# A product of h moved to GpSimd and four casts of v moved to ScalarE in a fused retention and bilinear feed-forward kernel

## The chip, the core and the metric

The kernel runs on one core of a Trainium2 chip. The metric is device time in microseconds (us) of one execution. The five engines run their own instruction streams and meet through semaphores: TensorE (PE in the rows, with its weight loads as PEld), VectorE (DVE), ScalarE (ACT), GpSimd (POOL) and the queue of SyncE (SP), which issues DMA transfers here.

## The reference

```python
gamma = 1.0 - 2.0 ** (-5.0 - np.arange(H))         # q, k, v: 4 x 8 heads x 768 x 64
for t in range(S):
    state = gamma * state + outer(k[t], v[t])
    y[t] = q[t] @ state / sqrt(D)
x = y.transpose(0, 2, 1, 3).reshape(3072, 512)
out = ((x @ w_a) * (x @ w_b)) @ w_out              # w_a, w_b: 512 x 1536, w_out: 1536 x 512
```

Inputs and output are float32. The kernel multiplies in bf16 and accumulates in float32.

## The kernel before, in words

**Slots.** The 3072 rows of x are 24 slots of 128 tokens, six per batch. For a slot, GpSimd scales k and q by a decay table (`kqb`, line 292) and SP transposes the result by DMA (`kqT`, line 333). The cast of v to bf16 is `vb`; GpSimd does it for most slots (line 251), ScalarE for slots 12 to 19 (`v_cast`, line 249). `turn(new, old)` takes slots in pairs: the state update (`st`, line 394, reads `kqb` and `vb`), the scores (`at`, line 376, masked by VectorE into `aT`, line 382), and, for the older pair, the two products that give y (lines 414 and 424), which ScalarE copies to `xt` (line 435).

**Tiles.** The feed-forward part takes the slots in seven tiles, J = 0 to 6, of 4, 2, 2, 2, 2, 4 and 8 slots. For a tile, `xt` meets twelve blocks `ft` of 128 columns of w_a and of w_b. A plain block (`ffn_a`, `ffn_g`) takes four matmuls into a PSUM bank `a`, which ScalarE copies to `asb` (line 575), and four into a bank `g`; VectorE then multiplies `g` by `asb` into `ht` (line 586), which is h. The banks come from a ring of three in strict rotation, which the scores of one slot of a pair also use, so the first product of the block behind a turn takes the bank of the `g` ahead of it. The product of h with w_out, and some of the first products, are done in a Strassen-like form with seven half products p1 to p7 instead of eight: class `Group` for w_out (banks mA, mB, mC, sums of h in `hs`), `Unit` for the last tile, and `Quad` for the sixth.

**The sixth tile** is J = 5, slots 14 to 17. Its blocks 0, 6 and 1, 7 are two "halved pairs". Pair p = 0 is `a` (w_a) and `b` (w_b), pair p = 1 is `c` and `d`. A half product leaves its bank through `Quad.leave`. For w_a, VectorE adds the bank to a saved copy (`snapf`, line 965) and writes `asb`. For w_b, it adds likewise into `ht` and then multiplies `ht` by `asb` in place. That last multiplication goes to VectorE for i = 0 (once per pair, in p2) and to GpSimd for i = 1 (twice per pair, in p5 and p4). Blocks 2 and 3 are plain ones (F2, G2, F3, G3).

**Order.** Everything is issued in the order of the code, each engine in its own order. The sixth tile's pairs stand in a string, `LACED`, between the halved w_out product of tile 4 (the `m` steps). Around the place of the change it reads

```python
... V18 L20 m3 c1 d1 F3 H3 c2 d2 c6 d6 c7 d7 c5 d5 m4 c3 d3 V19 c4 d4 G3
```

`V18` is `v_cast(18)`, and `L20` is `late_v(20)`, GpSimd's casts of v of slots 20 and 21. `H3` is a sum of h. Behind the string come `late_kq(22)` (the scaled k and q of slots 22 and 23), `turn(18, 16)`, blocks 4, 5 and 8, `turn(20, 18)`, blocks 9, 10 and 11, `turn(22, 20)`, and `big()`, the last tile. The sums of h for the sixth tile's w_out product are named by three digits, s, a and b: `hsum(5, s, a, b)`. `sums(5, ft)` issues those that belong behind block ft (`WHEN`): "324" behind block 4, "102", "402" and "346" behind block 5, "224d" and "124" behind 9, "424" behind 10, and "246", "146", "446" behind 11. `blocks(J, a, b)` calls it for all blocks but its last one; "324" goes to VectorE, the others to GpSimd (a "d" means VectorE). `weight_pieces` are sums of weight blocks for the last tile (`wsa`, `wsb`) on GpSimd.

Of the kernel before, what the change touches and what calls it, by code (L numbers as in the profile page):

```python
# [12 lines left out]
ALU = mybir.AluOpType  # L13
# [9 lines left out]
       "S02 S01 b7 a2 b2 S04 a6 b6 S13 a5 b5 S12 a3 b3 a4 b4 S11 c7 d7 c6 d6 S14 c5 d5 "  # L23
       "c3 c4 d4 d3")
V_LATE = range(12, 20)
LACED = ("X3 X2 m1 m7 m2 a1 b1 a2 b2 m6 X1 a6 b6 a7 b7 F2 X4 m5 a5 b5 K20 G2 a3 b3 a4 b4 V18 L20 "
         "m3 c1 d1 F3 H3 c2 d2 c6 d6 c7 d7 c5 d5 m4 c3 d3 V19 c4 d4 G3")
LOADS = "p0 p1 w0 w1 a1 b1 a2 k2 q2 b2 v2 o0 o1 o2 o3 o4 o5 s6 t8".split()

# [2 lines left out]
def kernel(  # L32
# [10 lines left out]
    nc = tc.nc  # L43
# [7 lines left out]
    NFT = DFF // P  # L51
# [51 lines left out]
    def seq(bi):  # L103
        ins = bi.ins
        prev = last.get(ins.engine)
        if prev is not None:
            tc.add_manual_dep(ins, prev.name, nosync, reason="program order")
        last[ins.engine] = ins
        return bi
# [5 lines left out]
    raws, wst, whole = {}, {}, {}  # L115

    def load_slot(t, names="kqv"):
        b, ci = divmod(t, NCH)
        for nm in names:
            src = {"k": k, "q": q, "v": v}[nm]  # L120
            if nm == "q":
                if t % 2 == 0:
                    load_two(nm, src, b, ci // 2, t)
                continue
            if t % 2 == 0:
                whole[nm] = raw_tile([P, 2, H, D], F32, nm + "f", nm + "f")
            raws[nm, t] = whole[nm][:, t % 2]
            s = src[b, :, ci * P : (ci + 1) * P, :].rearrange("h p d -> p h d")
            seq(nc.sync.dma_start(out=raws[nm, t], in_=s))
# [117 lines left out]
    def cast(engine, dst, src):  # L247
        if engine is nc.scalar:
            seq(nc.scalar.copy(dst, src))
        else:  # L250
            seq(engine.tensor_copy(dst, src))  # L251
# [19 lines left out]
    kb, qb, vb, kqT, aT = {}, {}, {}, {}, {}  # L271
# [27 lines left out]
    def casts(t, between=lambda: None):  # L299
        new_nat(t)  # L300
        scaled(nc.gpsimd, t, 0)
        between()
        scaled(nc.gpsimd, t, 1)
        if t not in range(12, 20):
            cast(nc.gpsimd, vb[t], raws["v", t])
        u = t + 2
        if u == 20:
            load_slot(u, "kq")
        flip(t)
        if u == 20:  # L310
            load_slot(u + 1, "k")
            return
        if u == 21:
            load_slot(u - 1, "v")
            load_slot(u, "v")
            load_slot(22, "kq")
            return
        if u in V_LATE:
            if u == 13:
                load_slot(12, "q")  # L320
            elif u == 19:
                load_slot(18, "kq")
            load_slot(u, {12: "k", 18: ""}.get(u, "kq"))
            if u % 2:
                load_slot(u - 1, "v")
                load_slot(u, "v")
        elif u < NSLOT:
            load_slot(u)
# [8 lines left out]
    def late_kq(t):  # L337
# [5 lines left out]
        if t == 20:  # L343
            load_slot(23, "k")
            load_slot(22, "v")
            load_slot(23, "v")

    def late_v(t):
        for u in (t, t + 1):
            cast(nc.gpsimd, vb[u], raws["v", u])  # L350

    def casts_two(t):
        for u in (t, t + 1):
# [74 lines left out]
    def leave(t):  # L428
        J, i = where[t]
        key, i = (J, i) if J < BIG else ((J, i // 4), i % 4)  # L430
        if i == 0:
            pool, tag = (wstage, "w") if key == (BIG, 1) else (xtp, "xt")
            xt[key] = pool.tile([P, KT, 4 * P], BF16, tag=tag, name="xt")
        for r in range(2):
            seq(nc.scalar.copy(xt[key][:, 2 * r : 2 * r + 2, i * P : (i + 2) * P],
                               ys[t // 2][r].rearrange("p j a s n -> p j (a s n)")))
# [127 lines left out]
    def ffn_a(J, ft, c0=0, c1=None):  # L564
        c1 = TILES[J] * P if c1 is None else c1
        if J not in ht:
            ht[J] = htp.tile([P, NFT, 4 * P], BF16, tag="ht", name="ht")
        fs = slice(ft * P, (ft + 1) * P)
        bank = psff.tile([P, 4 * P], F32, tag="ff", name="a")
        a = bank[:, : c1 - c0]  # L570
        for kt in range(KT):
            seq(nc.tensor.matmul(a, wa_bf[:, kt, fs], xcols(J, kt, c0, c1),  # L572
                                 start=(kt == 0), stop=(kt == KT - 1)))
        asb = asbs[J, ft, c0] = asbp.tile([P, 4 * P], BF16, tag="asb", name="asb")[:, : c1 - c0]
        seq(nc.scalar.copy(asb, a))  # L575
        psff.back(bank)

    def ffn_g(J, ft, c0=0, c1=None):
        c1 = TILES[J] * P if c1 is None else c1
        fs = slice(ft * P, (ft + 1) * P)  # L580
        bank = psff.tile([P, 4 * P], F32, tag="ff", name="g")
        g = bank[:, : c1 - c0]
        for kt in range(KT):
            seq(nc.tensor.matmul(g, wb_bf[:, kt, fs], xcols(J, kt, c0, c1),  # L584
                                 start=(kt == 0), stop=(kt == KT - 1)))
        seq(nc.vector.tensor_tensor(ht[J][:, ft, c0:c1], g, asbs.pop((J, ft, c0)), op=ALU.mult))  # L586
        psff.back(bank)

    def ffn_ab(J, ft):
        store()  # L590
        ffn_a(J, ft)
        ffn_g(J, ft)
# [3 lines left out]
    def store():  # L596
        for dst, src in held:
            seq(nc.sync.dma_start(out=dst, in_=src))
        held.clear()
# [21 lines left out]
    def tt(dst, x, y, op, eng=nc.vector):  # L621
        seq(eng.tensor_tensor(dst, x, y, op=op))  # L622
# [23 lines left out]
    def hsum(J, s, a, b, eng=nc.vector):  # L646
        U = slice(int(J == 0), 2 if isinstance(J, tuple) else TILES[J] // 2)
        hs_tile(J, s)
        v = ht[J].rearrange("p (k j) (u r n) -> p r k j u n", k=2, r=2, n=P)
        A11, A12, A21, A22 = (v[:, r, k2, a:b, U] for r in range(2) for k2 in range(2))  # L650
        S = {x: hs[J, x][:, a:b, U] for x in (1, 2, 3, 4) if (J, x) in hs}
        x, y, op = {3: (A11, A21, ALU.subtract), 2: (A22, S[3], ALU.subtract), 1: (A21, A22, ALU.add),
                    4: (A12, S.get(2), ALU.subtract)}[s]
        tt(S[s], x, y, op, eng)
# [8 lines left out]
    def sums(J, ft, eng=nc.vector):  # L663
        for what in WHEN.get(ft, []):
            hsum(J, *map(int, what[:3]), nc.vector if what[3:] else eng)
# [105 lines left out]
    def laced(order):  # L771
        made = {"m": Group(4, 0, Y0, AT0, Y1)}
        for p in range(2):
            made.update({"ac"[p]: Quad(p, "a", AT1, "kqT2"), "bd"[p]: Quad(p, "b", Y1, "aT")})
        ht[5] = htp.tile([P, NFT, 4 * P], BF16, tag="ht", name="ht")
        for x in order.split():
            if x[0] == "H":
                hsum(5, int(x[1]), 0, 1)
            elif x[0] in "XFGVKL":
                {"X": xf_sum, "F": lambda f: (store(), ffn_a(5, f)), "G": lambda f: ffn_g(5, f), "V": v_cast,  # L780
                 "K": late_kq, "L": late_v}[x[0]](int(x[1:]))
            else:
                getattr(made[x[0]], "p" + x[1])()

# [147 lines left out]
    class Quad:  # L932
# [40 lines left out]
        def leave(self, i, c, bank, n):  # L973
            cols = slice(c * DH, (c + 1) * DH)
            if self.w == "a":
                tt(self.half(i)[:, cols], self.bank[bank], self.snaps[n], ALU.add)
                return
            h = ht[5][:, NP * i + self.p, cols]
            tt(h, self.bank[bank], self.snaps[n], ALU.add)
            tt(h, h, self.half(i)[:, cols], ALU.mult, nc.vector if i == 0 else nc.gpsimd)  # L980

        def p1(self):
            self.A = self.whole(FF)
# [64 lines left out]
    D_, G_, A_ = nc.vector, nc.gpsimd, nc.scalar  # L1048
    K, Q = 0, 1
# [75 lines left out]
    def blocks(J, a, b):  # L1125
        for ft in range(a, b):
            ffn_ab(J, ft)
            if J == 5 and ft + 1 < b:
                sums(J, ft, G_ if ft > 8 else nc.vector)
        if J == 5 and b == 6:  # L1130
            sums(J, 5, G_)

# [7 lines left out]
    def v_cast(t):  # L1140
        cast(nc.scalar, vb[t], raws["v", t])
# [26 lines left out]
    weight_pieces(4)  # L1168
    casts(11)
    blocks(2, 3, 6)  # L1170
    hsum(2, 3, 0, 6, G_)
    blocks(2, 6, 7)
    turn(8, None)
    casts(12, lambda: three(2, 7))
    hsums(2, 0, 3, G_)
    blocks(2, 10, 11)
    turn(10, 8)
    blocks(2, 11, NFT)
# [38 lines left out]
    hsums(4, 3, 6, G_)  # L1217
    casts(19)
    laced(LACED)
    hsum(5, 3, 1, 2, G_)  # L1220
    hsum(5, 2, 0, 2, G_)
    late_kq(22)
    turn(18, 16)
    late_v(22)
    blocks(5, 4, 6)
    blocks(5, 8, 9)
    weight_pieces(2)
    turn(20, 18)
    sums(5, 8, G_)
    blocks(5, 9, NFT)  # L1230
    turn(22, 20)
    sums(5, NFT - 1, G_)
    weight_pieces(8)
# [31 lines left out]
```

## Time and profile before

| | |
|---|---|
| time, median of 3 runs | 219.09 us (218.52 to 219.52) |
| time of the profiled execution | 218.49 us |
| its span, first to last instruction | 216.8 us |
| granted TensorE clock | 1.00 throughout |
| busy: PE, DVE, ACT, POOL | 97%, 69%, 47%, 72% of the span |
| chain that ended last | 89% PE |

The profiled execution's time is 1.69 us more than its span, and 0.60 us below the median. In the timeline rows the columns are the start in us, the busy time from the first start to the last end of the instructions that the row merges, the engine, the line, the operation, what is written and read, the shape, and the count. Matmuls overlap, since a new one starts while the one ahead is still draining. Two of 256 columns are shown with 0.38 us, though the next pair starts 0.22 us after them. So a wait of TensorE is read from the distance of starts, not from the busy time.

### The profile page before, as it was taken

To read this page: it belongs to the slowest core of one execution; us is meant where nothing else is said; L and a number is where in the kernel's file an instruction comes from. 1 tells how busy PE (TensorE), PEld (TensorE's weight loads), DVE (VectorE), ACT (ScalarE), POOL (GpSimd) and SP (SyncE) were. 2 spreads that over 40 slices of the span, in tenths; PEclk is the share of its full clock that TensorE was granted. 3 is DMA by queue.
4 is the path that set the end of the run, shared out by engine and by line. 5 is a ranking of instruction groups with operands and counts; after the bars stand their busy time and mean duration, and the time that the engine had idled before them with its cause. 6 is when DMAs were issued, how large, how long until landed. Compare 5 with 4: busy or idle time off the path is not lost.

```text
span 216.8 us, 5705 instructions
## 1 busy us (share of the span) xinstructions
PE 210.4 (97%) x2240; PEld 146.4 (68%) x2252; DVE 149.2 (69%) x273; ACT 102.8 (47%) x231; POOL 155.4 (72%) x187
## 2 busy tenths in 40 slices
PE   7989999999999999999999999999999999999994
PEld 3558445587458888888888877456864444458883
DVE  3776346845984486356377979686577987688962
ACT  3256325343224444465576475446546656652331
POOL 5265876879776849989879979999997999530000
DMA  5999999999999999999979999960013000000055
GB/s 162 290 321 364 384 317 358 384 266 232 186 237 246 197 238 223 197 206 275 200 148 261 243 207 210 243 131 3 3 52 143 0 0 3 2 0 0 27 194 169
DMA packets 85162, 39.68 MB, mean 183 GB/s; under 512 B 57488, under 2 KB 78864, under 8 KB 85136
## 3 DMA queue, kind: packets, MB, share of 16 engines
q1 hardware_dynamic: 84992, 39.26, 78.1%
q8 instruction: 17, 0.28, 0.5%
q10 hardware_dynamic: 144, 0.07, 0.1%
q14 instruction: 9, 0.07, 0.1%
HBM read 28.31 MB, written 6.29 MB: 160 GB/s over the span
## 4 chain that ended last, share of the span: by engine, by line
PE 89%; SPq 3%; DMA 3%; DVE 1%; issue 1%; ACT 1%; POOL 0%; ACTq 0%
PE a L572 18%; PE g L584 18%; PE mA L689 12%; PE uA L863 9%; PE mB L689 6%; PE o L609 5%; PE uB L863 4%; SPq L138 3%; DMA wsta<-in_moe_w_a_dram 3%; PE mC L689 3%; PE at L376 2%; PE uC L863 2%; PE y L424 2%; PE st L394 2%; PE fa L953 2%; PE fb L953 1%
## 5 line engine op out<-in xcount | busy, mean ns | idle before, releaser
L586 DVE TENSOR_TENSOR ht<-g,asb 128x256 bf16<-128x256 f32 (+1 forms) x70 | 34.4, 493 | 31.1 <-PE g L584 28.0
L572 PE MATMUL a<-xt,wa_bf 128*128 128x256 bf16 (+1 forms) x277 | 48.4, 299 | 0.2
L584 PE MATMUL g<-xt,wb_bf 128*128 128x256 bf16 (+1 forms) x279 | 48.2, 300 | 0.1
L575 ACT CAST asb<-a 128x256 bf16<-128x256 f32 (+1 forms) x70 | 30.0, 429 | 34.8 <-PE a L572 33.2
L584 PEld LDWEIGHTS <-wb_bf 128*128 128x128 bf16 x280 | 27.0, 98 | 10.2
L572 PEld LDWEIGHTS <-wa_bf 128*128 128x128 bf16 x280 | 26.5, 98 | 10.7 <-POOL wa_bf L251 0.4
L292 POOL TENSOR_TENSOR kqb<-kf,ktab 128x512 bf16<-128x512 f32 x22 | 23.3, 1062 | 7.2 <-DMA kf<-in_k_dram 4.3
L870 ACT COPY snap<-uA 128x512 f32<-128x512 f32 x36 | 20.0, 588 | 15.4 <-PE uA L863 13.0
L689 PEld LDWEIGHTS <-hs 128*128 128x128 bf16 x234 | 22.8, 98 | 3.6
L292 POOL TENSOR_TENSOR kqb<-qf,qtab 128x512 bf16<-128x512 f32 x18 | 19.2, 1065 | 4.8 <-DMA qf<-in_q_dram 4.8
L382 DVE TENSOR_TENSOR aT<-at,mask 128x512 bf16<-128x512 f32 x36 | 22.3, 682 | 0.3
L622 POOL TENSOR_TENSOR ht<-gsb,asb 128x512 bf16<-128x512 bf16 x13 | 15.2, 1173 | 7.0 <-DVE gsb L622 6.9
L696 ACT COPY snaps<-mA 128x256 f32<-128x256 f32 x30 | 11.0, 374 | 18.9 <-PE mA L689 18.9
L689 PEld LDWEIGHTS <-ht 128*128 128x128 bf16 x180 | 17.5, 98 | 3.2
L622 POOL TENSOR_TENSOR hs<-ht 128x384 bf16<-128x384 bf16 (+3 forms) x14 | 15.8, 1132 | 2.1 <-DVE ht L586 2.1
L622 POOL TENSOR_TENSOR hs<-ht,hs 128x384 bf16<-128x384 bf16 (+1 forms) x17 | 16.8, 994 | 0.6 <-DVE ht L586 0.5
L689 PE MATMUL mA<-wsum,hs 128*128 128x256 bf16 x120 | 15.2, 273 | 0.0
L251 POOL CAST vb<-vf 128x512 bf16<-128x512 f32 x16 | 9.8, 633 | 6.7 <-DMA vf<-in_v_dram 6.7
L622 DVE TENSOR_TENSOR osb<-mB,snaps 128x256 f32<-128x256 f32 x20 | 8.4, 421 | 8.2 <-ACT snaps L696 4.4
L609 PE MATMUL o<-wo_bf,ht 128*128 128x512 bf16 x46 | 10.6, 379 | 0.1
L622 DVE TENSOR_TENSOR gsb<-uB,snap 128x512 bf16<-128x512 f32 x12 | 8.2, 686 | 2.9 <-ACT snap L870 2.1
L622 DVE TENSOR_TENSOR asb<-uB,snap 128x512 bf16<-128x512 f32 x12 | 8.2, 685 | 2.9 <-ACT snap L870 2.0
(138 smaller groups left out, 373.4 us busy)
## 6 DMA issues: line engine op xcount, KB each, us to landing
qf<-in_q_dram SPq DMA_DIRECT2D x12, 512.0 KB, 6.1
out_dram<-osb SPq DMA_DIRECT2D x21, 256.0 KB, 4.2
kf<-in_k_dram SPq DMA_DIRECT2D x18, 256.0 KB, 5.0
vf<-in_v_dram SPq DMA_DIRECT2D x18, 256.0 KB, 5.1
wsta<-in_moe_w_a_dram SPq DMA_DIRECT2D x6, 512.0 KB, 7.7
wsto<-in_moe_w_out_dram SPq DMA_DIRECT2D x6, 512.0 KB, 8.7
wstb<-in_moe_w_b_dram SPq DMA_DIRECT2D x5, 512.0 KB, 8.3
kf<-in_k_dram SPq DMA_DIRECT2D x3, 512.0 KB, 7.1
```

Source lines behind the costliest of these rows:

```text
L292: seq(eng.tensor_tensor(dst, src, tab, op=ALU.mult))
L382: seq(nc.vector.tensor_tensor(aT[t][:, r], at[r], mask.to_broadcast([P, HP, P]), op=ALU.mult))
L572: seq(nc.tensor.matmul(a, wa_bf[:, kt, fs], xcols(J, kt, c0, c1), start=(kt == 0), stop=(kt == KT - 1)))
L575: seq(nc.scalar.copy(asb, a))
L584: seq(nc.tensor.matmul(g, wb_bf[:, kt, fs], xcols(J, kt, c0, c1), start=(kt == 0), stop=(kt == KT - 1)))
L586: seq(nc.vector.tensor_tensor(ht[J][:, ft, c0:c1], g, asbs.pop((J, ft, c0)), op=ALU.mult))
L609: seq(nc.tensor.matmul(o, ht[J][:, ft, i * P : (i + 1) * P], wo_bf[:, ft], start=(ft == 0), stop=(ft == NFT - 1), skip_group_check=True))
L622: seq(eng.tensor_tensor(dst, x, y, op=op))
L689: seq(nc.tensor.matmul(m, w, right[:, j], start=(first and j == 0), stop=(j == NP - 1), skip_group_check=True))
L696: seq(nc.scalar.copy(self.snaps[:, n], self.bank["A"]))
L863: seq(nc.tensor.matmul(m, w, right[:, k], start=(first and k == 0), stop=(k == 1), skip_group_check=True))
L870: seq(nc.scalar.copy(self.snaps[n], self.bank["A"]))
```

## The change

One multiplication moves from VectorE to GpSimd: that of `d2`, the step p2 of pair p = 1 for w_b. Four casts of v, slots 20 to 23, move from GpSimd to ScalarE, each behind the copy of one plain block (4, 5, 9 and 11). To make room for the calls, `blocks(5, 4, 6)` and `blocks(5, 9, NFT)` are cut in two, which moves the sum "324" from behind block 4 to behind block 5, behind the calls of the three sums of block 5.

```diff
-LACED = ("... K20 G2 a3 b3 a4 b4 V18 L20 "
+LACED = ("... K20 G2 a3 b3 a4 b4 V18 "
          "m3 c1 d1 F3 H3 c2 d2 c6 d6 c7 d7 c5 d5 m4 c3 d3 V19 c4 d4 G3")
...
-    def late_v(t):
-        for u in (t, t + 1):
-            cast(nc.gpsimd, vb[u], raws["v", u])
...
             h = ht[5][:, NP * i + self.p, cols]
             tt(h, self.bank[bank], self.snaps[n], ALU.add)
-            tt(h, h, self.half(i)[:, cols], ALU.mult, nc.vector if i == 0 else nc.gpsimd)
+            tt(h, h, self.half(i)[:, cols], ALU.mult, nc.vector if (i, self.p) == (0, 0) else nc.gpsimd)
...
+        if (J, b) == (5, 10):
+            sums(J, 9, G_)
         if J == 5 and b == 6:
             sums(J, 5, G_)
...
     late_kq(22)
     turn(18, 16)
-    late_v(22)
-    blocks(5, 4, 6)
+    blocks(5, 4, 5)
+    v_cast(20)
+    blocks(5, 5, 6)
+    sums(5, 4)
+    v_cast(21)
     blocks(5, 8, 9)
     weight_pieces(2)
     turn(20, 18)
     sums(5, 8, G_)
-    blocks(5, 9, NFT)
+    blocks(5, 9, 10)
+    v_cast(22)
+    blocks(5, 10, NFT)
+    v_cast(23)
     turn(22, 20)
```

VectorE's order from the step c2 to the step d4. Before, `ht<-ht,asb` is the product of d2, and the two rows ahead of it are the additions of c2 and d2:

```order
L622 TENSOR_TENSOR asb<-fa,snapf 128x256
L622 TENSOR_TENSOR ht<-fa,snapf 128x256
L622 TENSOR_TENSOR ht<-ht,asb 128x256
L622 TENSOR_TENSOR asb<-fa,snapf 128x256
L622 TENSOR_TENSOR ht<-fb,snapf 128x256
L622 TENSOR_TENSOR osb<-mB,snaps 128x256
L622 TENSOR_TENSOR ht<-fb,asb 128x256
```

With the change (its lines stand four lower in number here):

```order
L618 TENSOR_TENSOR asb<-fa,snapf 128x256
L618 TENSOR_TENSOR ht<-fa,snapf 128x256
L618 TENSOR_TENSOR asb<-fa,snapf 128x256
L618 TENSOR_TENSOR ht<-fb,snapf 128x256
L618 TENSOR_TENSOR osb<-mB,snaps 128x256
L618 TENSOR_TENSOR ht<-fb,asb 128x256
```

The product is gone, so the additions of c5 and d5 follow those of c2 and d2 at once.

GpSimd's order over the same steps and up to the sums of block 5, before (the first row is the last of the scalings of slots 20 and 21):

```order
L292 TENSOR_TENSOR kqb<-qf,qtab 128x2x4x64
L622 TENSOR_TENSOR ht<-ht,asb 128x256
L251 CAST vb<-vf 128x512 x2
L622 TENSOR_TENSOR ht<-ht,asb 128x256 x2
L622 TENSOR_TENSOR hs_2601<-ht 128x256
L622 TENSOR_TENSOR hs_2662<-ht,hs_2601 128x512
L292 TENSOR_TENSOR kqb<-kf,ktab_175 128x2x4x64
L292 TENSOR_TENSOR kqb<-qf,qtab 128x2x4x64
L292 TENSOR_TENSOR kqb<-kf,ktab_175 128x2x4x64
L292 TENSOR_TENSOR kqb<-qf,qtab 128x2x4x64
L251 CAST vb<-vf 128x512 x2
L622 TENSOR_TENSOR hs_2803<-ht 128x512
```

and with the change:

```order
L292 TENSOR_TENSOR kqb<-qf,qtab 128x2x4x64
L618 TENSOR_TENSOR ht<-ht,asb 128x256 x4
L618 TENSOR_TENSOR hs_2599<-ht 128x256
L618 TENSOR_TENSOR hs_2660<-ht,hs_2599 128x512
L292 TENSOR_TENSOR kqb<-kf,ktab_175 128x2x4x64
L292 TENSOR_TENSOR kqb<-qf,qtab 128x2x4x64
L292 TENSOR_TENSOR kqb<-kf,ktab_175 128x2x4x64
L292 TENSOR_TENSOR kqb<-qf,qtab 128x2x4x64
L618 TENSOR_TENSOR hs_2799<-ht 128x512
```

The four casts are gone, and one product more stands behind that of b4.

VectorE's order from block 4 to the turn behind block 8, before (`hs_2601<-ht` is the sum "324"):

```order
L586 TENSOR_TENSOR ht<-g,asb 128x512
L622 TENSOR_TENSOR hs_2601<-ht 128x512
L586 TENSOR_TENSOR ht<-g,asb 128x512 x2
L382 TENSOR_TENSOR aT<-at_2835,mask 128x512
L382 TENSOR_TENSOR aT<-at_2836,mask 128x512
```

and with the change:

```order
L582 TENSOR_TENSOR ht<-g,asb 128x512 x2
L618 TENSOR_TENSOR hs_2599<-ht 128x512
L582 TENSOR_TENSOR ht<-g,asb 128x512
L378 TENSOR_TENSOR aT<-at_2833,mask 128x512
L378 TENSOR_TENSOR aT<-at_2834,mask 128x512
```

The sum now stands between the products of blocks 5 and 8.

More of the change, by code (lines that the diff above doesn't have):

```diff
@@ L25 @@
 V_LATE = range(12, 20)
-LACED = ("X3 X2 m1 m7 m2 a1 b1 a2 b2 m6 X1 a6 b6 a7 b7 F2 X4 m5 a5 b5 K20 G2 a3 b3 a4 b4 V18 L20 "
+LACED = ("X3 X2 m1 m7 m2 a1 b1 a2 b2 m6 X1 a6 b6 a7 b7 F2 X4 m5 a5 b5 K20 G2 a3 b3 a4 b4 V18 "
          "m3 c1 d1 F3 H3 c2 d2 c6 d6 c7 d7 c5 d5 m4 c3 d3 V19 c4 d4 G3")
@@ L778, in laced @@
                 hsum(5, int(x[1]), 0, 1)
-            elif x[0] in "XFGVKL":
+            elif x[0] in "XFGVK":
                 {"X": xf_sum, "F": lambda f: (store(), ffn_a(5, f)), "G": lambda f: ffn_g(5, f), "V": v_cast,
-                 "K": late_kq, "L": late_v}[x[0]](int(x[1:]))
+                 "K": late_kq}[x[0]](int(x[1:]))
             else:
```

## Prediction

> **What bounds the kernel now.** I read the page first, then the busy time by stage, then the timelines of the engines around the change.
>
> ```profile
> span 216.8 us, 5705 instructions
> PE 89%; SPq 3%; DMA 3%; DVE 1%; issue 1%; ACT 1%; POOL 0%; ACTq 0%
> 10.00:120.00 110.00, 109.33 (x1359) 81.41 (x1359) 70.34 (x130) 51.11 (x120) 86.25 (x102) 1.00 1.15 263
> 120.00:150.00 30.00, 29.77 (x384) 19.84 (x387) 24.71 (x46) 16.44 (x39) 28.12 (x32) 1.00 0.90 179
> 150.00:213.60 63.60, 63.28 (x442) 40.63 (x446) 48.57 (x78) 32.17 (x67) 36.94 (x37) 1.00 0.12 42
> ```
>
> The second line is the chain that ended last: 89% of the span is TensorE's own work, and GpSimd holds 0% of it. The stage rows (length, then PE, PEld, DVE, ACT, POOL busy) say the same by place. The change acts between 120 and 150 us. There TensorE is busy for 29.77 of 30.00 us, while GpSimd is at 28.12 and VectorE at 24.71. From 150 us to the last product TensorE is at 63.28 of 63.60. So relief for GpSimd or VectorE is worth only what TensorE waits for them. GpSimd looks full, but that alone costs nothing.
>
> Busy time can hide short waits, so I looked for them in the distances of TensorE's starts.
>
> ```profile
> 131.15 0.38 PE L953 MATMUL fa<-xt,wea 128*128 128x256 bf16 x2
> 131.37 0.38 PE L953 MATMUL fb<-xt,web 128*128 128x256 bf16 x2
> 131.72 0.38 PE L953 MATMUL fa<-xf,wa_bf 128*128 128x256 bf16 x2
> 132.04 0.38 PE L953 MATMUL fb<-xf,wb_bf 128*128 128x256 bf16 x2
> ...
> 130.22 1.10 DVE L622 TENSOR_TENSOR ht<-ht,asb 128x256 bf16<-128x256 bf16 x1
> 131.25 0.41 DVE L622 TENSOR_TENSOR asb<-fa,snapf 128x256 bf16<-128x256 f32 x1
> 131.59 0.41 DVE L622 TENSOR_TENSOR ht<-fb,snapf 128x256 bf16<-128x256 f32 x1
> ```
>
> A pair of half products takes 0.22 us: 131.15 to 131.37. But c4 starts 0.35 us after d3 (131.37 to 131.72) and d4 another 0.32 us later: waits of 0.13 and 0.10, together 0.23 us. Both reuse a bank that VectorE still has to read. The read for c4 ends at 131.25 + 0.41 = 131.66, that for d4 at 131.59 + 0.41 = 132.00, each some 0.05 us ahead of the product. VectorE is late there because of the product of d2 in the row at 130.22, the one that the change takes away. I found no other wait of TensorE of this kind up to the end; what is left are steps of about 0.1 us where the shape of the products changes.
>
> **The change, part by part.**
>
> *The product of d2.* VectorE loses the row at 130.22 with its 1.10 us.
>
> ```profile
> 130.45 0.37 ACT L965 COPY snapf<-fa 128x256 f32<-128x256 f32 x1 [0.23 <-PE fa L953]
> 130.72 0.38 ACT L965 COPY snapf<-fb 128x256 f32<-128x256 f32 x1
> ```
>
> The addition of c5 then waits for ScalarE's copy instead, which ends at 130.82; that of d5 for 131.10. So the reads end near 130.87 + 0.41 = 131.28 and 131.21 + 0.41 = 131.62. Without waits c4 would start at 131.59 and d4 at 131.81. Both reads are done by then, with 0.31 and 0.19 us to spare, so the whole 0.23 us goes. What is late next is ScalarE's copy, which follows TensorE at a fixed distance and doesn't hold it.
>
> *The product on GpSimd.*
>
> ```profile
> 130.14 1.04 POOL L292 TENSOR_TENSOR kqb<-qf,qtab 128x512 bf16<-128x512 f32 x1
> 131.14 0.71 POOL L622 TENSOR_TENSOR ht<-ht,asb 128x256 bf16<-128x256 bf16 x1
> 131.80 1.17 POOL L251 CAST vb<-vf 128x512 bf16<-128x512 f32 x2
> 132.93 1.30 POOL L622 TENSOR_TENSOR ht<-ht,asb 128x256 bf16<-128x256 bf16 x2
> 138.46 1.04 POOL L292 TENSOR_TENSOR kqb<-kf,ktab 128x512 bf16<-128x512 f32 x1 [0.37 <-DMA kf<-in_k_dram]
> 139.47 1.04 POOL L292 TENSOR_TENSOR kqb<-qf,qtab 128x512 bf16<-128x512 f32 x1
> 140.45 1.17 POOL L251 CAST vb<-vf 128x512 bf16<-128x512 f32 x2
> 141.58 1.16 POOL L622 TENSOR_TENSOR hs<-ht 128x512 bf16<-128x512 bf16 x1
> ```
>
> The product takes about 0.65 us here (1.30 for two) and stands at 131.80 in place of two casts, which held 1.13 us up to the next start. So what follows comes some 0.5 us earlier, until the scaling at 138.46, which waits for a load of k and does not move. At 140.45 the other two casts go, and the sums start there instead of 141.58, 1.13 us earlier. Queued behind the product are those of d5 and d4, two sums and the scalings of slots 22 and 23, none of them later than before. GpSimd's lead is worth nothing by the stage rows: TensorE waits for it nowhere. I count 0.
>
> *The casts on ScalarE.* Here is the engine they move to, with the copies that they stand behind or ahead of.
>
> ```profile
> 131.83 0.62 ACT L249 CAST vb<-vf 128x512 bf16<-128x512 f32 x1
> 136.08 0.59 ACT L575 CAST asb<-a 128x512 bf16<-128x512 f32 x1
> 137.81 0.59 ACT L575 CAST asb<-a 128x512 bf16<-128x512 f32 x1 [1.14 <-PE a L572]
> 139.48 0.59 ACT L575 CAST asb<-a 128x512 bf16<-128x512 f32 x1 [1.08 <-PE a L572]
> 142.99 0.59 ACT L575 CAST asb<-a 128x512 bf16<-128x512 f32 x1
> 144.66 0.59 ACT L575 CAST asb<-a 128x512 bf16<-128x512 f32 x1 [1.09 <-PE a L572]
> 146.39 0.59 ACT L575 CAST asb<-a 128x512 bf16<-128x512 f32 x1 [1.14 <-PE a L572]
> 148.29 0.37 ACT L249 CAST gst<-st 128x256 bf16<-128x256 f32 x1 [1.32 <-PE st L394]
> ...
> 140.24 0.32 PE L394 MATMUL st<-vb,kqb 128*64 128x64 bf16 x8
> 147.94 0.32 PE L394 MATMUL st<-vb,kqb 128*64 128x64 bf16 x8
> ```
>
> A cast takes 0.62 us and falls into idle time of 1.14, 1.08, 1.09 and 1.32 us ahead of the next instruction, so it ends about 0.5 us before that one is due. If that cover were gone, the rest of the cast would push the copy, and with it the product of the block. Their data is there: GpSimd read v of slots 20 and 21 from 131.80 on, of 22 and 23 from 140.45 on, and ScalarE comes to them after about 136.7, 138.4, 143.6 and 147.0. Their readers are the state updates at 140.24 and 147.94, after casts that end near 137.3 and 139.0 for the one, near 144.2 for the other; slot 23 is read later still. Cost 0.
>
> The Trainium skill (SBUF — State Buffer, section "Who interferes with whom") says that ScalarE waits for no other engine at its SBUF ports; the 0.62 us above, taken while GpSimd casts from 131.80, agrees.
>
> *The sum "324".* It moves behind the product of block 5 on VectorE.
>
> ```profile
> 137.57 0.80 DVE L622 TENSOR_TENSOR hs<-ht 128x512 bf16<-128x512 bf16 x1
> 138.69 0.69 DVE L586 TENSOR_TENSOR ht<-g,asb 128x512 bf16<-128x512 f32 x1 [0.32 <-PE g L584]
> 140.41 0.69 DVE L586 TENSOR_TENSOR ht<-g,asb 128x512 bf16<-128x512 f32 x1 [1.03 <-PE g L584]
> 141.86 1.04 PE L572 MATMUL a<-xt,wa_bf 128*128 128x512 bf16 x3
> 144.66 0.58 DVE L622 TENSOR_TENSOR hs<-ht,hs 128x512 bf16<-128x512 bf16 x1
> ```
>
> It took 0.80 us, and the room between the two products is 140.41 − 138.69 − 0.69 = 1.03. Its reader is the sum at 144.66, 5 us later. GpSimd's scaling from 138.46 to 139.50 stands beside it. The pair at 130 shows what that does: VectorE's product began at 130.22 under GpSimd's row from 130.14 to 131.18 and ended at 131.32, 0.14 us after it. So "324" may end as late as about 139.5 + 0.3 = 139.8, still ahead of the product of block 8, due at 140.41 − 0.23 = 140.18. Cost 0, with the far end below as a rival. No DMA and no queue of SP changes its order.
>
> **Sum.** −0.23 + 0 + 0 + 0 = −0.23 us. Against the profiled execution: 218.49 − 0.23 = 218.26. That execution lies 0.60 below the median of 219.09, so as a median 218.86. Bounds of the terms: the gain lies between 0 (below) and 0.3, if the steps of 0.1 us near it shrink too.
>
> **Rivals.**
>
> *A. Nothing arrives.* The 0.23 us is met again by the next wait, for a bank, a mask or the load of k at 138.46. A turn, with its masks and banks, follows right behind d4 and G3. Against it: no TensorE distance up to the end is longer than its shape asks for, so nothing stands ready to take it. Time 218.49, as a median 219.09.
>
> *B. GpSimd's lead counts.* If TensorE waited for sums of h that GpSimd brings 1.13 us earlier, the gain would be 0.23 + 1.13 = 1.36 us: 217.13, as a median 217.73. For it: GpSimd is busy for 28.12 of 30 us. Against: 0% of the chain, and 63.28 of 63.60 behind it.
>
> *C. "324" is locked out (slower).* From 138.46 on GpSimd runs without a pause: scalings to 139.50 and 140.51, then, with the change, sums to about 141.6 and 142.7. If VectorE lost against each new one, "324" would end near 139.8, 140.8, 141.9 or 143.0, and the product of block 8 about 0.65 later. TensorE's row at 141.86, due at 141.63, takes that product's bank. One or two losses cost nothing, and three decide: 142.53 − 141.63 = +0.9, net +0.67 (as a median 219.76). Four cost +2.0, net +1.8 (220.9). Against it: the product at 130.22 got in after one GpSimd instruction.
>
> The Trainium skill (the same page and section) states the lock as a rule: a VectorE instruction with two SBUF inputs and a GpSimd one that reads SBUF shut each other out, and the second waits for the whole of the first. The row at 130.22 agrees; by that rule as it stands, one loss is the likely case and C costs nothing.
>
> *D. A cause that the rows don't show*, such as a stall in fetching instructions on engines whose streams change length: +1.2 or more, 220.3 or above.
>
> **How the numbers follow.** Chances: the forecast 0.69, A 0.12, B 0.07, C 0.08 (0.03 at three losses, 0.05 at four or more), D 0.04. About 0.5% (1.1 us) is what a measurement of this kernel can tell from no change. Within it lie the forecast, A and C at three: 0.84. Faster by more: B, 0.07. Slower by more: C at four and D, 0.09. The three runs shown reach from 0.57 below their median to 0.43 above it. The forecast with that spread is 218.3 to 219.3, A 218.5 to 219.5, C at three 219.8. The range 218.0 to 219.7 holds the first two whole, with some tenths for another chip, and leaves out B, D and most of C, fewer than 2 in 10.
>
> **What would show it.** Right: c4 and d4 start 0.22 us after the product ahead; the last product ends 0.2 us earlier; "324" ends before 140.2; ScalarE's copies of blocks 5, 8, 10 and 11 keep their distance to TensorE. Wrong: a TensorE row behind a turn that starts late with VectorE's product just ahead of it (C), a hole in GpSimd's or ScalarE's stream that no semaphore explains (D), or TensorE rows from 150 on that close up by more than 0.3 us (B).

## The result, and the profile after

The changed kernel takes 218.27 us (median of 20 runs, 218.16 to 218.52), against 218.81 us for the kernel before in as many runs (218.34 to 219.52). The ratio is 0.9974, with a 95% interval of 0.9966 to 0.9982. It is faster by a quarter of a per cent, which lies within the 0.5%. The profiled execution took 218.28 us with a span of 216.6.

So two numbers have to be explained. The median fell by 0.54 us. The shortest run fell by 0.18 and the profiled span by 0.2, about the 0.23 us of the prediction. The rest of the median goes with the spread: 9 of the 20 runs before were above 218.9 us, none of the changed kernel's. Such longer executions are what the experiments are about.

The stages of the changed kernel, in the columns of the prediction's first rows (length, then PE, PEld, DVE, ACT, POOL busy):

```profile
120.00:150.00 30.00, 29.98 (x389) 20.02 (x388) 23.74 (x45) 18.51 (x43) 27.49 (x29) 1.00 0.91 179
150.00:213.60 63.60, 63.49 (x446) 40.52 (x444) 48.35 (x79) 32.28 (x67) 36.16 (x37) 1.00 0.12 43
```

VectorE has 1.0 us less, GpSimd 0.6 less and ScalarE 2.1 more between 120 and 150 us. (The trace of before lacks some records of TensorE, 384 products against 389, so its busy time isn't compared.)

The timeline of TensorE and VectorE at the place of d2's product, after:

```profile
131.39 0.38 PE L949 MATMUL fb<-xt,web 128*128 128x256 bf16 x2
131.61 0.38 PE L949 MATMUL fa<-xf,wa_bf 128*128 128x256 bf16 x2
131.83 0.38 PE L949 MATMUL fb<-xf,wb_bf 128*128 128x256 bf16 x2
...
129.79 0.41 DVE L618 TENSOR_TENSOR ht<-fa,snapf 128x256 bf16<-128x256 f32 x1
130.88 0.42 DVE L618 TENSOR_TENSOR asb<-fa,snapf 128x256 bf16<-128x256 f32 x1 [0.67 <-ACT snapf L961]
131.22 0.41 DVE L618 TENSOR_TENSOR ht<-fb,snapf 128x256 bf16<-128x256 f32 x1
```

c4 and d4 (second and third row) each start 0.22 us behind the product ahead, and VectorE now waits for ScalarE's copy, as forecast. Set row against row, TensorE is 0.02 us later than before up to d3, 0.11 earlier at c4, 0.22 earlier at d4, and 0.22 earlier at every row from there to the end.

GpSimd, ScalarE and the moved sum, after:

```profile
131.18 2.65 POOL L618 TENSOR_TENSOR ht<-ht,asb 128x256 bf16<-128x256 bf16 x4
138.40 1.04 POOL L292 TENSOR_TENSOR kqb<-kf,ktab 128x512 bf16<-128x512 f32 x1 [0.71 <-PE g L580]
139.40 1.23 POOL L292 TENSOR_TENSOR kqb<-qf,qtab 128x512 bf16<-128x512 f32 x1
140.59 1.15 POOL L618 TENSOR_TENSOR hs<-ht 128x512 bf16<-128x512 bf16 x1
147.88 1.16 POOL L618 TENSOR_TENSOR hs<-ht,hs 128x512 bf16<-128x512 bf16 x1 [0.23 <-DVE ht L582]
...
136.35 0.62 ACT L249 CAST vb<-vf 128x512 bf16<-128x512 f32 x1
137.59 0.59 ACT L571 CAST asb<-a 128x512 bf16<-128x512 f32 x1 [0.62 <-PE a L568]
...
139.08 0.64 DVE L618 TENSOR_TENSOR hs<-ht 128x512 bf16<-128x512 bf16 x1
140.20 0.69 DVE L582 TENSOR_TENSOR ht<-g,asb 128x512 bf16<-128x512 f32 x1 [0.47 <-PE g L580]
```

The scaling at 138.40 still waits (the releaser that the row names is the latest event; before, the same instruction waited for the load of k). The sums behind it start at 140.59 instead of 141.58, 0.99 us earlier and not 1.13: the scaling beside "324" took 1.23 us where it took 1.04 before. The sum at 147.88, the "246" behind block 11, now waits 0.23 us for VectorE: GpSimd has caught up. ScalarE's copy of block 5 still waits 0.62 us for TensorE behind the cast. "324" takes 0.64 us and ends at 139.72.

### The profile page after: what moved, and what is told of

Read it like the earlier page. It is cut to its first block, busy times and chain, and to the rows that moved or that the text cites. A ratio compares the mean times of both kernels' runs of the same rounds, so it can differ in the third digit from the quotient of the medians.

```text
span 216.6 us, 5713 instructions
## 1 busy us (share of the span) xinstructions
PE 210.7 (97%) x2252; PEld 146.1 (67%) x2252; DVE 147.5 (68%) x272; ACT 104.9 (48%) x235; POOL 154.2 (71%) x184
## 4 chain that ended last, share of the span: by engine, by line
PE 91%; SPq 3%; DMA 3%; POOL 0%; issue 0%; DVE 0%
PE a L568 18%; PE g L580 18%; PE mA L685 12%; PE uA L859 10%; PE mB L685 6%; PE o L605 5%; PE uB L859 5%; SPq L138 3%; DMA wsta<-in_moe_w_a_dram 3%; PE mC L685 3%; PE at L372 2%; PE uC L859 2%; PE y L420 2%; PE st L390 2%; PE fa L949 2%; PE fb L949 1%
## 5 line engine op out<-in xcount | busy, mean ns | idle before, releaser
L251 POOL CAST vb<-vf 128x512 bf16<-128x512 f32 x12 | 7.5, 641 | 6.7 <-DMA vf<-in_v_dram 6.7
```

## The experiments

Theory one: VectorE's product of d2 also makes the longer executions. Theory two: they come from a place that the change doesn't touch. Theory three came out of the first set: in some executions SP's loads are late, GpSimd falls behind, and TensorE waits for it near 151 us. The edits are made to the kernel before, but for the third of set 3, the whole change with the early load, which is made to the changed one.

Each ratio is the record's own, to executions of the kernel before taken beside the set, and is not the quotient of the two medians. Those executions had a median of 218.63 us in set 1 (12 of 34 above 218.9), 218.78 in set 2 (13 of 29) and 218.69 in set 3 (4 of 23).

**Set 1, the parts alone.** First the kernel before again.

> The kernel before once more, for other executions of it. Its 20 runs spread from 218.34 to 219.52 us, those of the changed kernel only from 218.16 to 218.52, and the medians differ by 0.54 us where the two traces differ by 0.22. Theory one (VectorE's product of d2 meets GpSimd differently from run to run): if the profiled execution is one of the longer ones, c4 or d4 starts more than 0.35 us behind the product ahead of it. Theory two (the spread comes from a place that the change doesn't name, the start or the tail): c4 and d4 wait 0.13 and 0.10 us as before, and the extra time stands elsewhere. Ratio 1.000.

Median 218.62 us of 12 runs (218.46 to 219.57, three above 218.9), ratio 0.9996 (0.998 to 1.0012). The profiled execution was a short one, and c4 and d4 wait there as before.

The product of d2 alone:

```diff
-            tt(h, h, self.half(i)[:, cols], ALU.mult, nc.vector if i == 0 else nc.gpsimd)
+            tt(h, h, self.half(i)[:, cols], ALU.mult, nc.vector if (i, self.p) == (0, 0) else nc.gpsimd)
```

> Only the product of d2 moves to GpSimd; all four casts stay on GpSimd and the sum 324 stays behind block 4. By the prediction's sum the whole 0.22 us is here: c4 and d4 start 0.22 us after the pair ahead, time 218.3, and by theory one the spread goes too (all runs within 218.2 to 218.6, ratio 0.9975). By the rival that GpSimd needs the room that the casts leave, GpSimd is 0.65 us later from 133 us on, and the gain is partly lost: 218.5 or more.

Median 218.70 us (218.16 to 219.32), ratio 0.9986 (0.9969 to 1.0004). The shortest runs are those of the changed kernel, but three of 12 are above 218.9. The profiled one took 218.95. Its timeline of TensorE, then of GpSimd:

```profile
131.39 0.38 PE L953 MATMUL fb<-xt,web 128*128 128x256 bf16 x2
131.61 0.38 PE L953 MATMUL fa<-xf,wa_bf 128*128 128x256 bf16 x2
131.83 0.38 PE L953 MATMUL fb<-xf,wb_bf 128*128 128x256 bf16 x2
150.68 0.60 PE L689 MATMUL mA<-wsum,hs 128*128 128x256 bf16 x4
151.76 0.39 PE L689 MATMUL mA<-wsum,hs 128*128 128x256 bf16 x2 [0.49 <-POOL hs L622]
...
139.54 1.04 POOL L292 TENSOR_TENSOR kqb<-kf,ktab 128x512 bf16<-128x512 f32 x1 [0.66 <-DMA kf<-in_k_dram]
142.78 0.61 POOL L251 CAST vb<-vf 128x512 bf16<-128x512 f32 x1 [0.64 <-ACT xt L435]
149.44 2.27 POOL L622 TENSOR_TENSOR hs<-ht,hs 128x512 bf16<-128x512 bf16 x2
```

The 0.22 us is won at c4 and d4, so it is the product's, and theory one is dead for the spread: long executions stay without that product on VectorE. At 151 us TensorE waits. It has done four of the six products with the sums `hs` (150.68, due to go on at 151.12) and gets the last two at 151.76, behind "246" (the second of the two sums in the row at 149.44), which ends at 149.44 + 2.27 = 151.71. That is 0.65 us, three times the gain. In front of it GpSimd had waited 0.66 us for the load of k of slot 23 and 0.64 before the cast of v of slot 23. The product that it gained did not make it late: that stands ahead of the load of k, and GpSimd still had 0.66 us to wait behind it.

The casts alone (on ScalarE in the places of the change, with "324" left behind block 4):

> Only the four casts move to ScalarE; the product of d2 stays on VectorE and the sum 324 stays behind block 4. By the prediction's sum nothing comes: waits of c4 and d4 as before (0.13 and 0.10 us), ratio 1.000, spread of before. By the rival that GpSimd's lead counts, or that GpSimd's casts make the spread, the time falls to 218.3 and the runs close up.

Median 218.57 us, ratio 0.9987 (0.9974 to 1.0001), and all 12 runs between 218.46 and 218.73. So the expected "nothing" was half right: the shortest run isn't shorter, but the long ones are gone (12 of 34 beside them).

"324" alone:

```diff
-    blocks(5, 4, 6)
+    blocks(5, 4, 5)
+    blocks(5, 5, 6)
+    sums(5, 4)
```

> Only the sum 324 moves behind block 5. By the prediction nothing comes of it: VectorE does it in the 1.0 us before the product of block 8, ratio 1.000. By the lock-out rival it ends behind 140.8 us and a TensorE row at the turn starts late: 0.7 us slower or more.

Median 219.10 us (218.37 to 220.03), ratio 1.0004 (0.9987 to 1.002). The profiled execution was a short one (218.49) and shows TensorE within 0.01 us of before from 62 us on. No lock-out. Seven of the 12 runs are above 218.9 (12 of 34 beside them), with no profile of one of them. Whether the moved sum makes such runs more frequent is open.

**Set 2, where the longer executions come from.**

```diff
-"... b4 V18 L20 m3 ..."
+"... b4 V18 m3 ..."
...
-    blocks(5, 4, 6)
+    blocks(5, 4, 5)
+    sums(5, 4)
+    v_cast(20)
+    blocks(5, 5, 6)
+    v_cast(21)
```

> Only the casts of slots 20 and 21 move to ScalarE. Theory three, from the product-only run: in some executions SP's loads come about 1 us later, GpSimd waits longer for the load of k of slot 23, and then its sum for the w_out product ends too late for TensorE near 151 us; this makes the long executions. Room that is made ahead of that load (here 1.1 us at 131.8) is eaten by the wait for it, so the long executions stay: some of 12 runs above 218.9, median like before. Theory one (the long executions come from VectorE's product of d2): the long executions stay as well. Rival four (any 1.1 us off GpSimd will do): they go.

Median 218.80 us (218.51 to 219.47), five of 12 above 218.9, ratio 0.9998 (0.9984 to 1.0013). Not any 1.1 us will do.

```diff
-    late_v(22)
...
-    blocks(5, 9, NFT)
+    blocks(5, 9, 10)
+    v_cast(22)
+    blocks(5, 10, NFT)
+    v_cast(23)
```

(`sums(5, 9, G_)` is called behind block 9, as in the change.)

> Only the casts of slots 22 and 23 move to ScalarE. They stand behind the load of k of slot 23, so by theory three the sums start 1.1 us earlier and the long executions go: all runs within 218.4 to 218.75, the shortest as before (c4 and d4 still wait 0.23 us). By theory one the long executions stay. By rival four they go here as with slots 20 and 21.

Median 218.50 us (218.38 to 218.87), none above 218.9, ratio 0.9976 (0.996 to 0.9991). One run lies above the expected 218.75. It is the profiled one, and TensorE is 0.37 us late from 18.6 us on, after VectorE's first scaling had waited 1.38 us for k (0.89 before); it loses nothing later. So the start is a second source of spread, which the change doesn't touch.

```diff
-            ... nc.vector if i == 0 else nc.gpsimd)
+            ... nc.vector if (i, self.p) == (0, 0) else nc.gpsimd)
...
     blocks(5, 8, 9)
-    weight_pieces(2)
     turn(20, 18)
...
-    weight_pieces(8)
+    weight_pieces(10)
```

> The product of d2 on GpSimd as in the change, all casts left on GpSimd, and GpSimd's two weight sums between the sums of h (1.5 us from 144.9 on) moved behind them. By theory three this makes the room at 151 us that the product alone lacked: c4 and d4 without waits, no wait at 151, runs within 218.15 to 218.5, as with the whole change. If it is the casts on GpSimd themselves (their waits for the loads of v) that count, long executions stay.

Median 218.27 us (218.18 to 218.47), none above 218.9, ratio 0.9969 (0.9956 to 0.9981): the times of the whole change, with no cast moved. So room ahead of "246" is enough, wherever the casts run. The profiled execution (218.28 us) tests it. GpSimd, then TensorE:

```profile
142.32 0.61 POOL L251 CAST vb<-vf 128x512 bf16<-128x512 f32 x1 [0.87 <-ACT xt L435]
147.52 2.26 POOL L622 TENSOR_TENSOR hs<-ht,hs 128x512 bf16<-128x512 bf16 x2
150.69 0.82 PE L689 MATMUL mA<-wsum,hs 128*128 128x256 bf16 x6
```

The cast of v of slot 23 had to wait 0.87 us and starts at 142.32, where it starts at 141.01 in the profile of before (the second cast of its row at 140.45). Yet "246" ends at 147.52 + 2.26 = 149.78, 1.35 us ahead of the two products that need it (due 0.44 us behind 150.69), and TensorE doesn't wait.

> The kernel before, one more look, in the hope of one of its long executions (about one in three is above 218.9). If it is one, theory three wants TensorE to start late near 151 us behind GpSimd's sum, theory one a longer wait of c4 or d4 near 131.7. If it is a short one, nothing new.

This execution was one of the longer ones, 218.91 us. TensorE, then GpSimd, of the kernel before in this execution:

```profile
131.42 0.38 PE L953 MATMUL fb<-xt,web 128*128 128x256 bf16 x2
131.78 0.38 PE L953 MATMUL fa<-xf,wa_bf 128*128 128x256 bf16 x2
132.12 0.38 PE L953 MATMUL fb<-xf,wb_bf 128*128 128x256 bf16 x2
150.96 0.60 PE L689 MATMUL mA<-wsum,hs 128*128 128x256 bf16 x4
151.72 0.39 PE L689 MATMUL mA<-wsum,hs 128*128 128x256 bf16 x2 [0.16 <-POOL hs L622]
...
139.80 1.04 POOL L292 TENSOR_TENSOR kqb<-kf,ktab 128x512 bf16<-128x512 f32 x1 [1.64 <-DMA kf<-in_k_dram]
142.82 0.61 POOL L251 CAST vb<-vf 128x512 bf16<-128x512 f32 x1 [0.42 <-DMA vf<-in_v_dram]
149.40 2.27 POOL L622 TENSOR_TENSOR hs<-ht,hs 128x512 bf16<-128x512 bf16 x2
```

c4 and d4 wait as in the short execution, and the same two products at 151 us are late: 151.72 where 151.40 was due, right behind "246" at 149.40 + 2.27 = 151.67. GpSimd had waited 1.64 us for k (0.37 in the short one) and 0.42 for v. The wait for v of slot 23 is the last of the two, so it is that load that sets the end of "246": the sum ends 8.85 us behind the start of this cast here, and in the short execution too (141.01 and 149.85, within 0.01 us). Without the 0.42 us it would have ended at 151.25, ahead of the due 151.40: by these rows the late load of k alone would have cost nothing. From 62 us to this place TensorE stands 0.05 to 0.07 us behind the short execution, from it to the end 0.41 behind.

SP's timeline in the short and in this execution shows most of why k comes late (the third row of each is the load of k of slot 23):

```profile
128.64 0.89 SPq L138 DMA_DIRECT2D qf<-in_q_dram  x1
129.64 5.06 SPq L333 DMA_TRANSPOSE kqT<-kqb  x2
134.76 0.57 SPq L129 DMA_DIRECT2D kf<-in_k_dram  x1
```

```profile
129.30 1.00 SPq L138 DMA_DIRECT2D qf<-in_q_dram  x1
130.41 5.21 SPq L333 DMA_TRANSPOSE kqT<-kqb  x2
135.68 0.57 SPq L129 DMA_DIRECT2D kf<-in_k_dram  x1
```

The load stands behind two transposes that hold SP for 5 us, and is issued 0.92 us later here, of the 1.34 us by which GpSimd's scaling starts later. The loads of v of slots 22 and 23 stand behind it.

**Set 3, the load of k ahead of the transposes.**

```diff
     def late_kq(t):
+        if t == 20:
+            load_slot(23, "k")
         for u in (t, t + 1):
...
         if t == 20:
-            load_slot(23, "k")
             load_slot(22, "v")
```

> The kernel before with one edit: SP issues the load of k of slot 23 ahead of the two transposes of slots 20 and 21, which hold SP for 5 us, instead of behind them. All casts stay on GpSimd and the product of d2 on VectorE. By theory three the wait of GpSimd for this load near 138.4 us (0.37 us in a short execution, 1.64 in a long one) goes, its sums come 0.4 to 1.6 us earlier, and the long executions go: 218.4 to 218.75, median 218.5. c4 and d4 still wait 0.23 us. If the loads of v, which stay behind the transposes, are as bad, some long executions remain.

Median 218.99 us (218.39 to 219.87), six of 12 above 218.9, ratio 1.001 (0.9995 to 1.0025). The expectation fell: GpSimd no longer waits for k in the profiled (short) execution, yet the long ones are no rarer (4 of 23 beside them).

> The same early load together with the product of d2 on GpSimd; no cast moves. By theory three the 0.22 us of the product and the loss of the long executions add up: 218.15 to 218.5, median 218.3, as with the whole change. If the casts have to leave GpSimd for this, long executions remain above 218.7.

Median 219.27 us of 7 runs (218.35 to 219.66), six above 218.9, ratio 1.0022 (1.0006 to 1.0038): slower than before, if only by 0.2%. This fell too. The profiled execution (219.21) has no wait at 151 us, but is 0.99 us late by 18.5 us:

```profile
6.87 1.04 PE L482 MATMUL tp<-ident,kqb 128*128 128x128 bf16 x8 [0.72 <-DVE kqb L292]
15.71 0.70 PE L557 MATMUL idle<-zero 128*128 128x256 f32 x2 [0.66 <-ACT kqT L249]
```

where before the second of these waits is 0.42. VectorE's first scaling waited 1.33 us for k there, 0.89 before.

> The whole change with the early load on top, as a version that could beat both. By theory three nothing is left to win at 151 us, since TensorE waits for GpSimd in none of the changed kernel's executions: median 218.3, as the changed kernel. If GpSimd's lead is worth more than the lost wait, 218.0 or less.

Median 218.24 us of 10 runs (218.14 to 218.41), ratio 0.9978 (0.9969 to 0.9987), against 0.9974 for the change: the same. One profile of each shows TensorE without a wait at 151 us; that the other executions have none is inferred from their small spread.

> The early load of k once more, for a look at one of its long executions (7 of 12 were above 219.0). If GpSimd's casts now wait for the loads of v, which stay behind the transposes, GpSimd shows a wait for vf near 140 to 142 us and TensorE one near 151. If the long executions come from the start, TensorE is late by 0.3 us or more before 20 us. A short execution tells neither.

This was a short execution, 218.56 us. (Six, not seven, of the 12 runs before it were above 219.0.) TensorE loses nothing in it, yet the wait for v is there. GpSimd, TensorE, then SP:

```profile
140.61 0.61 POOL L251 CAST vb<-vf 128x512 bf16<-128x512 f32 x1 [0.31 <-PE st L395]
142.46 0.61 POOL L251 CAST vb<-vf 128x512 bf16<-128x512 f32 x1 [1.24 <-DMA vf<-in_v_dram]
149.04 2.27 POOL L623 TENSOR_TENSOR hs<-ht,hs 128x512 bf16<-128x512 bf16 x2
150.92 0.83 PE L690 MATMUL mA<-wsum,hs 128*128 128x256 bf16 x6
...
130.06 1.99 SPq L129 DMA_DIRECT2D kf<-in_k_dram  x1
132.16 4.21 SPq L333 DMA_TRANSPOSE kqT<-kqb  x2
136.47 1.20 SPq L129 DMA_DIRECT2D vf<-in_v_dram  x2
```

GpSimd no longer waits for k, but 1.24 us for v of slot 23. "246" ends at 149.04 + 2.27 = 151.31, and the products that need it are due at 151.36: 0.05 us of room is left, where the profile of before has 1.5. So theory three named the wrong load. TensorE's wait behind "246" is as it says, but the load that GpSimd waits for last is that of v of slot 23. The early load of k doesn't bring it forward: the two loads of v are issued from 136.47 on here, from 135.42 on in the profile of before. In the four profiles with a wait for it (the product alone, the weight sums moved, the longer execution of before, and this one) the trace has this load landing between 142.17 and 142.67 us, and the cast starts 0.15 us later. In two of these four the row names ScalarE's copy to `xt` instead. In the profile of before the load lands at 140.53.

No longer execution of the early load alone has a profile. How many of its longer runs come from v, and how many from the start, stays open.

## Why the prediction was right

**c4, d4 and the product of d2.** Right within 0.01 us: 0.22 instead of 0.23, at the two places named, kept to the end. The product alone gives it.

**The product on GpSimd, counted at 0.** Right in the profiles of the change and of the product alone. Where the product moved alone, its time went into the wait for k, and "246" ended at 151.71, against 151.67 in the longer execution of before, which lacks that product. TensorE lost 0.65 us there and not 0.32 because it was itself ready 0.28 us earlier (151.12 against 151.40). So in such an execution the gain at c4 and d4 is lost again, and the product alone brought no lower median (218.70 us, against 218.63 beside it).

**GpSimd's lead, "worth nothing: TensorE waits for it nowhere".** This step failed. It was read from one execution with no wait, and that was taken for all. In that execution "246" ended at 147.58 + 2.27 = 149.85, and the two products that need it were due at 151.33. That is 1.5 us of room, and a cast of v of slot 23 that starts 1.81 us later (142.82 against 141.01) uses it up. I gave rival B 0.07 and 1.36 us. Its mechanism is what the longer execution of before shows, at 0.34 us, and not what the short ones show. Together with the sets that made room and lost the longer executions, this explains why the median fell by 0.54 us where the sum said 0.23. That 218.27 lies 0.6 below the 218.86 forecast is about half this, and half that the three runs shown had a median of 219.09, where twenty have 218.81. How much of the longest executions of before (up to 220.1 us in set 2) the wait makes is not shown, since only one at 218.91 has a profile.

**The range.** 218.0 to 219.7 us also held rival A, no change at all, so the median inside it says little for the reasoning; the starts of c4 and d4 do. That the two profiles differ by just the 0.22 us was luck in part: both executions were short ones.

**ScalarE's casts, counted at 0.** Right for TensorE: the instruction behind each cast starts only 0.57 to 0.80 us after the cast's end. What the sum left out is that the move also takes the wait for v of slot 23 off GpSimd, and ScalarE comes to that cast at 146.65 us.

**"324" and rival C.** Right in the trace: 0.64 us, ending 0.5 us before the product of block 8. VectorE did not lose here to one GpSimd instruction after another. The row at 130.22 that the prediction leans on shows less than a full shut-out, too: the product ended 0.14 us behind GpSimd's instruction, though the product of b2, with the same shape, took 0.41 us in all at 122.61. **Rival A** did not happen, and nothing of the kind of **D** shows in the changed kernel's profile. D's +1.2 us was worked out from no row.

## What to carry to other kernels

A trace without a wait says that an engine was in time, not by how much. For each hand-over near a place where work is added or removed, subtract the producer's end from the consumer's due start, and compare this room with how much the loads ahead of the producer move between executions. A median can then fall by more than any single trace of before and after shows. Look also at the waits that the producer already has: the 0.65 us that GpSimd gained with the product vanished in one. Room ahead of a load that the engine waits for is eaten by that wait, while the same room behind it stays. And where several loads stand in a row, it is the last one that counts: bringing k forward left v where it was.

## What the runs showed that I had not expected

Between executions of the same program, GpSimd's scaling behind the load of k of slot 23 started at 138.46 or 139.80 us, its cast of v of slot 23 at 141.01 or 142.82, and the first loads of the kernel alone shift TensorE by up to 0.99 us before 19 us. Four kernels that leave GpSimd 1.1 us or more of extra room behind those loads (the change, the casts alone, the casts of slots 22 and 23 alone, the weight sums behind the sums of h) had no run above 218.9 in 56, and the change with the early load none in 10. Of the two with the load of k ahead of the transposes and all casts on GpSimd, 12 of 19 were above it.
